# Late weight blocks by a list of products, and the loads of k, v and q one by one, in a fused attention and MLP kernel

## The chip, the cores and the metric

The kernel runs on one core of a Trainium2 chip. The metric is the device time of one execution in microseconds (us). Times of a kernel are medians of several runs; a profiled execution gives the trace.

## What is computed

The reference is linear attention with a normalisation, then two MLPs one behind the other, all in fp32 (cut to the lines that matter):

```python
kv  = einsum('bhsd,bhse->bhde', k, v)             # B=8, H=8, S=576, D=64
out = einsum('bhsd,bhde->bhse', q, kv)
att = out / sqrt(mean(out*out, -1) + 1e-6) * g_norm
x   = att as (4608, 512)
x   = (((x @ w1) * (x @ w2)) @ w3) @ w_out        # 512 -> 1024 -> 1024 -> 512
out = silu(x @ w_in) @ w_out2                     # 512 -> 2048 -> 512
```

## The kernel before

**Precision.** A matrix product runs as three passes of TensorE over operands split in a high and a low part: ScalarE makes the high part with a copy, VectorE the low part with a subtraction. The weights come from memory as packed words; two ScalarE operations and one VectorE operation unpack 128x512 of them.

**Two stages.** The first stage (trace, 73 to 469 us) works on token chunks `c` of 512. For the five chunks in `PLAIN` it runs the first MLP directly: 40 steps, each of two groups of 12 matmuls (`pa`, `pb`) and a third group for the second product (`x2ps`). Between the groups stand slots, six to a step, at which other work is begun (`event`, `att_step`, lines 669 to 700): the attention of the next chunks, that is `kv_load` and `q_load` (DMAs issued on SyncE), `kv_mm`, `att_a` and so on. The table `at_` (line 672) says how far behind the start of a chunk each part stands, in halves of which one is a slot; a chunk starts 27 slots after the last. Also in between, `pace` calls `advance` (line 299), one move of a pipeline that loads packed weights, splits them, forms sums of blocks and writes them to DRAM (`wbd`); its writes stand on SyncE's queue with a buffer of two tiles for each kind of sum.

The second stage (469 us to the end) runs the seven `UNITS`: units 0 and 1 (kind A) are the first MLP for the chunks that are left, units 2 to 6 (kind B) are the second MLP. Each matrix product is done by a seven-product scheme (Strassen-like): 52 blocks, seven products each, 12 matmuls in a product. In the text b2n3 is product 3 of block 2. The order of blocks is fixed by lines 710 to 715: unit 0's a0, b0, a1, b1, out0 are blocks 0 to 4, then unit 1's a0 (5), unit 0's out1 (6), unit 1's b0, a1, b1, out0 (7 to 10), unit 2's in0 (11), and so on.

**What a product waits for.** The results of a product land in PSUM; eight tiles go round, six to a block, two of them (one for each half `d`) for each of three banks. Products 0, 2, 4 and 6 use bank 0, product 1 bank 1, products 3 and 5 bank 2 (`RUNS`). Behind each product `post.after` has ScalarE copy a result out (products 0, 2, 3; in blocks of kind `a` also 6) or VectorE add it up. So ScalarE's copy of product 0 must be done before product 2 starts, that of 2 before 4, that of 3 before 5, and that of product 6 before product 1 of the next block, whose tiles are the same two. Every product also has a `w_load` behind it: SyncE waits until the product is done and refills its weight buffer, six products ahead of use.

**The late blocks.** Of the 16 blocks of the second MLP's weights, twelve are split in the first stage (`EARLY`) and four, 12 to 15, in the second stage, by the generator `late` (line 1009). It has eleven parts: (1) load the first half; (2) unpack it on ScalarE, two operations; (3) load the second half, finish the first on VectorE; (4) nothing; (5) unpack the second half on ScalarE; (6) finish it and form a sum on VectorE; (7) three more sums, one copy on ScalarE; (8) a copy and two low parts; (9) write four tiles, one copy and one low part; (10) another copy and low part, two writes; (11) the last two writes. The raw tile has one buffer (`LRAW`), the unpacked tiles `t0` and `t1` one each. `late_all` (line 1079) begins a block each seven parts (`LEVERY`), so that two blocks overlap in four parts; one part of each live block is issued ahead of each product in blocks whose name stands in `LATES`, that is blocks 0, 2, 4, 5 and the first products of 8.

The queues of the engines run in order: an instruction that waits holds up everything behind it on its engine.

Of the kernel before, what the change touches and what calls it, by code (L numbers as in the profile page):

```python
# [8 lines left out]
F32R = mybir.dt.float32r  # L9
U32 = mybir.dt.uint32  # L10
# [5 lines left out]
P = 128  # L16
B, H, S, D = 8, 8, 576, 64
# [5 lines left out]
N = 512  # L23
# [3 lines left out]
K2 = F2 // P  # L27
# [3 lines left out]
LATER = tuple(c for c in range(NCH) if c not in PLAIN)  # L31
UNITS = (("A", 512), ("A", 512), ("B", 512), ("B", 512), ("B", 512), ("B", 384), ("B", 384))
HMAX = max(w for _, w in UNITS)
HOP = 512
LRAW, LWH, LEVERY = 1, 3, 7
LATES = (("a", 0), ("a", 1), ("out", 0))
FIRST, PERIOD = 10, 13.5
EARLY = 12

NDB = {"A": K1 // 4, "B": K2 // 4}  # L40
WBD = {"in": 0, ("B", "out"): 4, "a": 8, "b": 10, ("A", "out"): 12}
# [38 lines left out]
def fused(ctx, tc, q, k, v, g, w1, w2, w3t, wo1, wb, out):  # L80
# [59 lines left out]
    for p in range(KD):  # L140
        r = 32 * p
# [455 lines left out]
    for x in ORDER.split():  # L597
        f = x.rstrip("0123456789")
# [26 lines left out]
        return [[(wch[4 * r + 2 * i + t][:, s], wcl[4 * r + 2 * i + t][:, s]) for r in range(2) for t in range(2)]  # L625
                for s in cols], wbd[WBD["A", "out"] + i][:, :, d]

    for n in range(K2):
        if n < EARLY:
            for role in range(3):  # L630
                pieces.append((wb[2 * n + role] if role < 2 else None, "block", role, wbd[n // 2][:, :, n % 2]))
        if n < 3 * K1 // 2:
            src, dst = resident(n)
            for role in range(3):
                pieces.append((src[role] if role < 2 else None, "sum", role, dst))
# [33 lines left out]
    def event(gap, f, *args):  # L669
        events.setdefault(int(2 * gap), []).append(lambda: f(*args))  # L670

    at_ = dict(k=4, q=7, a=4.5, a2=2.5, c=8, d=8.5, e=9.5, r=10.5)
    for c in range(1, NCH):
        gap = FIRST + PERIOD * (c - 2) - 4 * (c == B) if c > 1 else 1 - at_["a"]
        if 1 < c < B:
            event(gap, kv_mm, c, [0, 1, 2])
            event(gap, kv_load, c, [3, 4])
            event(gap + at_["k"], kv_mm, c, [3, 4])
            event(gap + at_["k"], kv_out, c)
        if c + 1 < B:  # L680
            event(max(gap + at_["k"], 2), kv_load, c + 1, [0, 1, 2])
        if c + 1 < NCH:
            for p in range(KD):
                event(gap + at_["q"], q_load, c + 1, p)
        for i in range(2):
            event(gap + at_["a"] + at_["a2"] * i, att_a, c, i)
            event(gap + at_["a"] + at_["a2"] * i, att_b, c, i)
        event(gap + at_["c"], att_c, c)
        event(gap + at_["d"], att_d, c)
        for f in (att_e, att_h, att_l):  # L690
            event(gap + at_["e"], f, c)
        for i in range(2):
            event(gap + at_["r"] + 2.5 * i, att_r, c, i)
            event(gap + at_["r"] + 2.5 * i, att_x, c, i)
            event(gap + at_["r"] + 2.5 + 2.5 * i + 0 * (c in LATER), att_f, c, i)

    def att_step(step, part):
        for n in range(6 * step + part - (part == 0), 6 * step + part + 1):
# [4 lines left out]
    def b_pool(name, **more):  # L703
        return ctx.enter_context(tc.tile_pool(name=name, **{**dict(bufs=1, reuse_waits="tile"), **more}))
# [10 lines left out]
    blocks.append((len(UNITS) - 1, "out", NDB[UNITS[-1][0]] - 1))  # L715
    stream = [(b, n) for b in range(len(blocks)) for n in range(7)]
    wt = {}

    def w_load(at):
        if at >= len(stream):  # L720
            return
        b, n = stream[at]
        u, which, i = blocks[b]
        from_ = w_rest if at % WBUFS else w_first
        t = from_.tile([P, 2, 2, 2 * P], F32, tag="w", name=f"w{b}_{n}")
        nc.sync.dma_start(out=t, in_=wbd[i + WBD[(UNITS[u][0], which) if which == "out" else which]][:, RUNS[n][1]])
        wt[b, n] = t
# [279 lines left out]
    lc = b_pool("lc")  # L1007

    def late(n):

        dst = wbd[n // 2][:, :, n % 2]

        def load(role):
            t = lc.tile([P, 2 * N], U32, tag="raw", bufs=LRAW, name=f"lraw{n}_{role}")
            nc.sync.dma_start(out=t, in_=wb[2 * n + role])
            return t.rearrange("p (n two) -> p n two", two=2)

        def scale(role, x):
            t = lc.tile([P, N], F32, tag=f"t{role}", name=f"lt{n}_{role}")
            z = lc.tile([P, N], U32, tag="wh", bufs=LWH, name=f"lz{n}_{role}")  # L1020
            nc.scalar.activation(out=t, in_=x[:, :, 1].bitcast(F32), func=AF.Prelu, scale=2.0 ** -112, alpha=-2.0 ** 32)
            nc.scalar.activation(out=z, in_=x[:, :, 0], func=AF.Copy, scale=0.93 * 2.0 ** -29)
            return t, z

        def bits(t, z):
            nc.vector.scalar_tensor_tensor(out=t.bitcast(U32), in0=t.bitcast(U32), scalar=3, in1=z,
                                           op0=ALU.logical_shift_left, op1=ALU.bitwise_or)

        def high(x):
            h = lc.tile([P, N], F32R, tag="wh", bufs=LWH, name=f"lh{n}")[:, :x.shape[-1]]  # L1030
            nc.scalar.copy(out=h, in_=x)
            return x, h

        def low(x, h):
            nc.vector.tensor_sub(out=x.bitcast(F32R), in0=x, in1=h.bitcast(F32))

        def write(op, x, h):
            o = x.shape[-1] // (2 * P)
            for i, y in ((0, h.bitcast(F32)), (1, x)):
                nc.sync.dma_start(out=dst[:, op:op + o, i, :], in_=y.rearrange("p (o c) -> p o c", c=2 * P))  # L1040

        raw = load(0)
        yield
        t0, z = scale(0, raw)
        yield
        raw = load(1)
        bits(t0, z)
        yield
        yield
        t1, z = scale(1, raw)  # L1050
        yield
        bits(t1, z)
        s12 = lc.tile([P, N], F32, tag="s12", name=f"ls12_{n}")
        s34 = lc.tile([P, N], F32, tag="s34", name=f"ls34_{n}")
# [12 lines left out]
        yield  # L1067
        write(A22, *x22)
        write(A11, *x1)
        x12 = high(s12)  # L1070
        low(*x12)
        yield
        x34 = high(s34)
        low(*x34)
        write(S1, *x12)
        yield
        write(S3, *x34)

    def late_all():
        todo = [late(n) for n in range(EARLY, K2)]  # L1080
        live = []
        at0 = 0
        while todo or live:
            if todo and at0 % LEVERY == 0:
                live.append(todo.pop(0))
            at0 += 1
            for x in list(live):
                if next(x, 0) == 0:
                    live.remove(x)
            yield  # L1090

    lates, LATE = late_all(), None
    gops = {}
    for b, (u, which, i) in enumerate(blocks):
        nxt = blocks[b + 1] if b + 1 < len(blocks) else None
        kind, w = UNITS[u]
        assert kind == "A" or (which, i) in (("in", 0), ("in", 1)) or LATE is not None
        post = {"in": Silu, "a": First, "b": Second, "out": Out}[which](b, u, i)
        ops = gops[u, i] if which == "out" else xops[u]
        more = u + 1 < len(UNITS)  # L1100
# [10 lines left out]
        if to_g:  # L1111
            gops[nxt[0], nxt[2]] = g_ops(nxt[0], nxt[2])
        for n in range(7):
            if (which, i) in LATES and next(lates, 0) == 0 and LATE is None:
                LATE = b
            if first and n < 3:
                ops.step(n + 4)
            if which == "out" and n + 3 < 7:
                ops.step(n + 3)
                if n + 3 == 6:  # L1120
                    held.append(ops.made[6])
            if steps and n >= 3:
                xops[u + 1].step(n - 3)
            if to_g:
                if n == (2 if first else 1):
                    for x in held:
                        nc.gpsimd.tensor_copy(out=gate, in_=x[:, 1, 0, :1].bitcast(F32))
                    held.clear()
                    gops[nxt[0], nxt[2]].sums()
                if n >= 4:  # L1130
                    gops[nxt[0], nxt[2]].step(n - 4)
            if n == sums_at:
                xops[u + 1].sums()
            if load:
# [57 lines left out]
```

## Time and profile before

| what | us |
|---|---|
| median of 3 runs (lowest to highest) | 1409.79 (1409.26 to 1409.94) |
| the profiled execution | 1409.83 |
| its span in the trace | 1408.0 |
| TensorE matmuls busy | 1378.2 |
| VectorE busy | 883.3 |
| ScalarE busy | 659.7 |
| GpSimd busy | 329.1 |

A busy share of an engine is a mean over both stages. Matmuls are pipelined, so that a busy TensorE is not one at its peak: the start-to-start time of its matmuls tells more. An engine's idle time ahead of an instruction is put down to what released it last.

### The profile page before, as it was taken

To read this page: it belongs to the slowest core of one execution; us is meant where nothing else is said; L and a number is where in the kernel's file an instruction comes from. 1 tells how busy PE (TensorE), PEld (TensorE's weight loads), DVE (VectorE), ACT (ScalarE), POOL (GpSimd) and SP (SyncE) were. 2 spreads that over 40 slices of the span, in tenths; PEclk is the share of its full clock that TensorE was granted. 3 is DMA by queue.
4 is the path that set the end of the run, shared out by engine and by line. 5 is a ranking of instruction groups with operands and counts; after the bars stand their busy time and mean duration, and the time that the engine had idled before them with its cause. 6 is when DMAs were issued, how large, how long until landed. Compare 5 with 4: busy or idle time off the path is not lost.

```text
span 1408.0 us, 19221 instructions
## 1 busy us (share of the span) xinstructions
PE 1378.2 (98%) x7012; PEld 1141.2 (81%) x7012; DVE 883.3 (63%) x1227; ACT 659.7 (47%) x1032; POOL 329.1 (23%) x206
## 2 busy tenths in 40 slices
PE   7999999999999999799999999999999999999998
PEld 4777777776778887688888888888888889999998
DVE  5854566567682476865774667545854576567458
ACT  5776445454552424522535354443535354544543
POOL 1000000000002040404532335124522442235222
PEclk9999999999999999999999999999999999999999
DMA  9755688988867497687677666866686668888886
GB/s 364 281 177 172 201 274 291 347 278 288 273 220 258 162 315 254 232 283 265 194 240 265 194 195 211 297 193 193 193 297 192 193 206 288 290 253 268 282 256 200
DMA packets 158157, 346.26 MB, mean 246 GB/s; under 512 B 15088, under 2 KB 73456, under 8 KB 158064
## 3 DMA queue, kind: packets, MB, share of 16 engines
q1 hardware_dynamic: 157488, 343.99, 74.1%
q8 instruction: 56, 0.92, 0.3%
q10 hardware_dynamic: 576, 1.05, 0.2%
q14 instruction: 37, 0.30, 0.1%
HBM read 270.53 MB, written 74.45 MB: 245 GB/s over the span
## 4 chain that ended last, share of the span: by engine, by line
PE 89%; DMA 5%; DVE 3%; ACT 2%; issue 1%; SPq 1%; DVEq 0%; ACTq 0%
PE ps L888 62%; PE wps L562 3%; PE pb L118 3%; PE x2ps L118 2%; PE pa L118 2%; PE pb L120 2%; PE pb L119 2%; PE x2ps L120 2%; PE x2ps L119 2%; PE pa L120 2%; PE pa L119 2%; PE kvps L342 1%; PE o L374 1%; DMA wbd<-w12l 1%; DMA v<-v_l 1%
## 5 line engine op out<-in xcount | busy, mean ns | idle before, releaser
L888 PE MATMUL ps<-xo,w 128*128 128x512 f32 (+1 forms) x2352 | 504.9, 375 | 8.9 <-ACT u L943 6.2
L888 PEld LDWEIGHTS ps<-xo,w 128*128 128x128 f32 x2352 | 433.8, 189 | 76.6 <-ACT u L943 7.0
L888 PE MATMUL ps<-go,w 128*128 128x512 f32 (+1 forms) x2016 | 426.2, 371 | 2.3 <-ACT c L991 1.3
L888 PEld LDWEIGHTS ps<-go,w 128*128 128x128 f32 x2016 | 368.4, 188 | 56.4 <-issue 2.0
L781 DVE TENSOR_TENSOR go<-g,go 128x1024 fp32r<-128x1024 f32 (+1 forms) x120 | 136.8, 1143 | 123.4 <-ACT go L780 122.1
L898 DVE TENSOR_TENSOR c<-ps,c 128x512 f32<-128x512 f32 (+1 forms) x280 | 170.8, 638 | 58.3 <-PE ps L888 56.1
L780 ACT CAST go<-g 128x1024 fp32r<-128x1024 f32 (+1 forms) x120 | 115.0, 978 | 50.6 <-PE ps L888 50.6
L768 POOL TENSOR_TENSOR x_t<-x2r 128x1024 f32<-128x1024 f32 (+1 forms) x14 | 32.6, 2329 | 436.1 <-DMA w<-wbd 435.6
L768 POOL TENSOR_TENSOR g_t<-g 128x1024 f32<-128x1024 f32 (+1 forms) x48 | 111.5, 2322 | 74.2 <-DVE g L970 69.3
L768 POOL TENSOR_TENSOR g<-g,g_t 128x1024 f32<-128x1024 f32 (+1 forms) x24 | 53.2, 2215 | 298.2 <-DVE go L781 298.2
L781 DVE TENSOR_TENSOR go<-g_t,go 128x1024 fp32r<-128x1024 f32 (+1 forms) x48 | 80.2, 1670 | 23.0 <-ACT go L780 23.0
L920 ACT COPY s<-ps 128x512 f32<-128x512 f32 (+1 forms) x40 | 21.7, 544 | 145.0 <-PE ps L888 145.0
L823 DVE TENSOR_TENSOR asb<-pb,asb 128x512 f32<-128x512 f32 x40 | 27.6, 690 | 84.0 <-PE pb L120 66.7
L898 DVE TENSOR_TENSOR g<-ps,s 128x512 f32<-128x512 f32 (+1 forms) x48 | 30.1, 642 | 68.0 <-PE ps L888 62.0
L113 ACT CAST ch<-asb 128x512 fp32r<-128x512 f32 x40 | 24.9, 624 | 92.6 <-DVE asb L823 92.6
L118 PE MATMUL x2ps<-ch,wch 128*128 128x512 f32 x160 | 65.0, 406 | 0.9 <-DVE x2o L655 0.9
L118 PE MATMUL pb<-xh,w12h 128*128 128x512 f32 x160 | 65.0, 406 | 0.0
L118 PE MATMUL pa<-xh,w12h 128*128 128x512 f32 x160 | 63.7, 398 | 0.0
L120 PE MATMUL x2ps<-ch,wcl 128*128 128x512 f32 x160 | 63.2, 395 | 0.0
L119 PE MATMUL x2ps<-cl,wch 128*128 128x512 f32 x160 | 63.0, 394 | 0.0
L120 PE MATMUL pb<-xh,w12l 128*128 128x512 f32 x160 | 62.5, 391 | 0.0
L119 PE MATMUL pb<-xl,w12h 128*128 128x512 f32 x160 | 62.4, 390 | 0.0
(139 smaller groups left out, 1760.4 us busy)
## 6 DMA issues: line engine op xcount, KB each, us to landing
w<-wbd SPq DMA_DIRECT2D x364, 512.0 KB, 4.4
wbd<-bh SPq DMA_DIRECT2D x60, 256.0 KB, 3.5
raw<-wb_l SPq DMA_DIRECT2D x24, 512.0 KB, 5.2
wbd<-s SPq DMA_DIRECT2D x48, 256.0 KB, 3.5
q<-q_l SPq DMA_DIRECT2D x36, 256.0 KB, 5.0
k<-k_l SPq DMA_DIRECT2D x32, 256.0 KB, 5.5
v<-v_l SPq DMA_DIRECT2D x32, 256.0 KB, 5.5
raw<-w_l SPq DMA_DIRECT2D x14, 512.0 KB, 4.5
```

The source lines that it names most:

```text
L113: nc.scalar.copy(out=h, in_=x)
L118: nc.tensor.matmul(out=ps_out, lhsT=ah, rhs=bh, start=first, stop=False)
L119: nc.tensor.matmul(out=ps_out, lhsT=ah, rhs=bl, start=False, stop=False)
L120: nc.tensor.matmul(out=ps_out, lhsT=al, rhs=bh, start=False, stop=last)
L562: nc.tensor.matmul(out=wps[m], lhsT=(l if which == "lh" else h)[:, x:x + P], rhs=rhs, start=left[m] == all_of, stop=left[m] == 1)
L768: nc.gpsimd.tensor_tensor(out=x, in0=x if a == place else self.src[a], in1=x if b == place else self.src[b], op=ALU.subtract)
L780: nc.scalar.copy(out=t[:, 0, :, :self.w], in_=x)
L781: self.cuts[n].tensor_tensor(out=t[:, 1, :, :self.w], in0=x, in1=t[:, 0, :, :self.w].bitcast(F32), op=ALU.subtract)
L823: nc.vector.tensor_mul(out=asb, in0=pb, in1=asb)
L888: mm = lambda a, bb, start, stop: nc.tensor.matmul(out=o, lhsT=a, rhs=bb, start=start, stop=stop, skip_group_check=True)
L898: eng.tensor_tensor(out=out_, in0=a, in1=b, op=ALU.add)
L920: nc.scalar.copy(out=t[nm, d], in_=o)
```

## The change

It has four parts. First, `LATES` becomes a list with a number for every product of the first blocks: so many parts of the late work are issued ahead of this product. Counted out, with the parts numbered on through each late block (part 11 of a block and part 1 of the next go together), the list gives:

| late block | part: product |
|---|---|
| 12 | 1: b0n0, 2: b0n2, 3: b0n3, 4 and 5: b0n4, 6: b1n0, 7: b1n1, 8: b1n2, 9: b1n6, 10: b2n1 |
| 13 | 1: b2n3, 2: b2n4, 3 and 4: b2n5, 5: b2n6, 6: b3n0, 7 and 8: b3n1, 9: b3n2, 10: b3n3 |
| 14 | 1: b4n4, 2: b6n2, 3 and 4: b6n6, 5: b7n3, 6: b8n0, 7: b8n1, 8: b8n5, 9: b8n6, 10: b9n0 |
| 15 | 1: b9n0, 2: b9n1, 3: b9n2, 4: b9n3, 5: b9n6, 6: b12n0, 7: b12n1, 8: b12n3, 9: b12n6, 10: b14n0, 11: b14n2 |

Second, `late_all` takes one late block at a time. Third, the order in which the first stage splits its twelve blocks becomes `NEED`; it is the same set of twelve, and the sums of resident tiles between them keep their places. Fourth, the loads of the attention move: in each chunk k and v of block 3 come 2 slots and those of block 4 come 4 slots after `kv_mm` of blocks 0 to 2 (both stood right behind it); blocks 0, 1 and 2 of the next chunk come 8, 10 and 12 slots after it (all stood at 8); q of pairs 0 and 1 comes at 17 slots and of pairs 2 and 3 at 22 (all stood at 14); the last part of the attention, `att_f`, comes one slot later. An assertion in `w_load` takes the place of the one in the block loop, and three named constants are written out as numbers.

```diff
-LRAW, LWH, LEVERY = 1, 3, 7
-LATES = (("a", 0), ("a", 1), ("out", 0))
+AT = dict(a=4.5, a2=2.5, k=4, l0=0, l1=1.0, l3=1, q=4.0, q1=0, c=8, d=8.5, e=9.5, r=10.5, r2=2.5, f=3.0)
+LATES = tuple(int(x) for x in """
+1011200 1110001 0101121 1211000 0000100 0000000
+0010002 0001000 1100011 2111001 0000000 0000000
+1101001 0000000 1010000 0011001 0100000 0100000
+0000000 0100000 0000000   
+""" if x.isdigit())
 EARLY = 12
+NEED = (0, 1, 2, 3, 8, 9, 4, 5, 10, 11, 6, 7, 12, 13, 14, 15)
...
-    for n in range(K2):
-        if n < EARLY:
+    for at_n, n in enumerate(NEED):
+        if at_n < EARLY:
...
+        n = at_n
...
-    at_ = dict(k=4, q=7, a=4.5, a2=2.5, c=8, d=8.5, e=9.5, r=10.5)
+    def place(c):
+        return FIRST + PERIOD * (c - 2) - 4 * (c == B)
...
             event(gap, kv_mm, c, [0, 1, 2])
-            event(gap, kv_load, c, [3, 4])
-            event(gap + at_["k"], kv_mm, c, [3, 4])
+            for i in range(2):
+                event(gap + AT["l3"] * (i + 1), kv_load, c, [3 + i])
+            event(gap + AT["k"], kv_mm, c, [3, 4])
...
-            event(max(gap + at_["k"], 2), kv_load, c + 1, [0, 1, 2])
+            for i in range(3):
+                event(max(gap + AT["k"] + AT["l0"] + AT["l1"] * i, 2), kv_load, c + 1, [i])
...
-                event(gap + at_["q"], q_load, c + 1, p)
+                event(gap + AT["a"] + AT["a2"] * (p // 2) + AT["q"] + AT["q1"] * (p % 2), q_load, c + 1, p)
...
-            event(gap + at_["r"] + 2.5 + 2.5 * i + 0 * (c in LATER), att_f, c, i)
+            event(gap + AT["r"] + AT["f"] + AT["r2"] * i, att_f, c, i)
...
     def late_all():
-        todo = [late(n) for n in range(EARLY, K2)]
-        live = []
-        at0 = 0
-        while todo or live:
-            if todo and at0 % LEVERY == 0:
-                live.append(todo.pop(0))
-            at0 += 1
-            for x in list(live):
-                if next(x, 0) == 0:
-                    live.remove(x)
-            yield
+        for n in NEED[EARLY:]:
+            yield from late(n)
+            undone.remove(n // 2)
...
         for n in range(7):
-            if (which, i) in LATES and next(lates, 0) == 0 and LATE is None:
-                LATE = b
+            for _ in range(LATES[7 * b + n] if 7 * b + n < len(LATES) else 0):
+                next(lates, None)
```

## Rows read from the trace of the kernel before

**Rows 1.** the page's busy time of TensorE over the span (part 1)

```profile
PE 1378.2 (98%) x7012; PEld 1141.2 (81%) x7012; DVE 883.3 (63%) x1227; ACT 659.7 (47%) x1032; POOL 329.1 (23%) x206
```

**Rows 2.** waits of TensorE by line: us in total, times, longest us

```profile
PE ps L888 <- ACT u L943: 6.2, 2, 5.6
...
PE rb L431 <- DVE rhl L421: 4.0, 3, 2.3
...
PE ps L888 <- DVE g L898: 2.7, 1, 2.7
...
PE kvps L342 <- DVE ob L438: 1.8, 2, 1.4
...
PE ps L888 <- ACT c L991: 1.3, 1, 1.3
...
PE x2ps L118 <- DVE x2o L655: 0.9, 1, 0.9
```

**Rows 3.** chain of work that ended last: start us, us, what

```profile
469.73 40.84 PE ps L888 x180
...
604.60 778.30 PE ps L888 x3720
...
1383.15 2.32 PE ps L888 x12
...
1385.67 18.98 PE ps L888 x108
```

**Rows 4.** windows: stretch, its us, busy us by engine, clock, DMA, GB/s

```profile
180.00:200.00 20.00, 17.72 (x70) 13.56 (x70) 15.66 (x28) 10.30 (x18) 0.00 (x0) 0.91 0.82 266
...
580.00:600.00 20.00, 13.12 (x44) 10.18 (x45) 15.91 (x18) 11.92 (x18) 4.85 (x3) 0.83 0.74 234
...
700.00:800.00 100.00, 100.00 (x443) 82.81 (x442) 59.99 (x67) 47.54 (x64) 27.52 (x13) 1.00 0.72 234
```

**Rows 5.** ScalarE timeline: start us, us, instruction [idle before <-releaser]

```profile
517.06 0.66 ACT L1021 ACTIVATE lt<-lraw 128x512 f32<-128x512 f32 x1 [5.36 <-DMA wbd<-lt]
...
523.23 0.68 ACT L1021 ACTIVATE lt<-lraw 128x512 f32<-128x512 f32 x1 [2.51 <-DMA lraw<-wb_l]
...
580.01 0.67 ACT L1021 ACTIVATE lt<-lraw 128x512 f32<-128x512 f32 x1 [6.50 <-DMA wbd<-lt]
...
583.54 1.06 ACT L943 COPY u<-ps 128x512 f32<-128x512 f32 x2
...
591.45 0.66 ACT L1021 ACTIVATE lt<-lraw 128x512 f32<-128x512 f32 x1 [5.87 <-DMA lraw<-wb_l]
```

**Rows 6.** the raw tile of the late blocks: its loads to landing

```profile
DMA to landing us min/median/max: 3.4/5.3/8.4
```

**Rows 7.** SyncE timeline, 170 to 176 us: start us, us, DMA issued

```profile
169.88 0.46 SPq L327 DMA_DIRECT2D k<-k_l  x1
...
174.03 0.33 SPq L327 DMA_DIRECT2D v<-v_l  x1
...
175.38 0.38 SPq L297 DMA_DIRECT2D wbd<-s  x1
```

**Rows 8.** VectorE timeline, 487 to 581: a quiet step, then steps beside GpSimd

```profile
487.05 0.42 DVE L1060 TENSOR_TENSOR ls<-lt,lt 128x256 f32<-128x256 f32 x1
...
572.73 2.62 DVE L1060 TENSOR_TENSOR ls<-lt,lt 128x256 f32<-128x256 f32 x1
...
575.60 5.38 DVE L1035 TENSOR_TENSOR lt<-lt,lh 128x256 fp32r<-128x256 f32 x2
```

**Rows 9.** costliest groups on the page: busy us, mean ns | idle before

```profile
L768 POOL TENSOR_TENSOR g_t<-g 128x1024 f32<-128x1024 f32 (+1 forms) x48 | 111.5, 2322 | 74.2 <-DVE g L970 69.3
```

**Rows 10.** VectorE timeline, 172 to 181 us

```profile
172.45 0.68 DVE L286 TENSOR_TENSOR s<-s,bh 128x512 fp32r<-128x512 f32 x1
...
180.90 0.42 DVE L253 TENSOR_TENSOR s<-t,t 128x256 f32<-128x256 f32 x1 [4.13 <-DMA wbd<-s]
```

**Rows 11.** DMA issues: count, KB each, median us to landing

```profile
k<-k_l SPq DMA_DIRECT2D x8, 128.0 KB, 3.7
```

More of the change, by code (lines that the diff above doesn't have):

```diff
@@ L670, in event @@
         events.setdefault(int(2 * gap), []).append(lambda: f(*args))
-    at_ = dict(k=4, q=7, a=4.5, a2=2.5, c=8, d=8.5, e=9.5, r=10.5)
+    def place(c):
+        return FIRST + PERIOD * (c - 2) - 4 * (c == B)
     for c in range(1, NCH):
-        gap = FIRST + PERIOD * (c - 2) - 4 * (c == B) if c > 1 else 1 - at_["a"]
+        gap = place(c) if c > 1 else 1 - AT["a"]
         if 1 < c < B:
             event(gap, kv_mm, c, [0, 1, 2])
-            event(gap, kv_load, c, [3, 4])
-            event(gap + at_["k"], kv_mm, c, [3, 4])
-            event(gap + at_["k"], kv_out, c)
+            for i in range(2):
+                event(gap + AT["l3"] * (i + 1), kv_load, c, [3 + i])
+            event(gap + AT["k"], kv_mm, c, [3, 4])
+            event(gap + AT["k"], kv_out, c)
         if c + 1 < B:
-            event(max(gap + at_["k"], 2), kv_load, c + 1, [0, 1, 2])
+            for i in range(3):
+                event(max(gap + AT["k"] + AT["l0"] + AT["l1"] * i, 2), kv_load, c + 1, [i])
         if c + 1 < NCH:
             for p in range(KD):
-                event(gap + at_["q"], q_load, c + 1, p)
+                event(gap + AT["a"] + AT["a2"] * (p // 2) + AT["q"] + AT["q1"] * (p % 2), q_load, c + 1, p)
         for i in range(2):
[L686 to L689, printed above, removed]
+            event(gap + AT["a"] + AT["a2"] * i, att_a, c, i)
+            event(gap + AT["a"] + AT["a2"] * i, att_b, c, i)
+        event(gap + AT["c"], att_c, c)
+        event(gap + AT["d"], att_d, c)
         for f in (att_e, att_h, att_l):
-            event(gap + at_["e"], f, c)
+            event(gap + AT["e"], f, c)
         for i in range(2):
-            event(gap + at_["r"] + 2.5 * i, att_r, c, i)
-            event(gap + at_["r"] + 2.5 * i, att_x, c, i)
-            event(gap + at_["r"] + 2.5 + 2.5 * i + 0 * (c in LATER), att_f, c, i)
+            event(gap + AT["r"] + AT["r2"] * i, att_r, c, i)
+            event(gap + AT["r"] + AT["r2"] * i, att_x, c, i)
+            event(gap + AT["r"] + AT["f"] + AT["r2"] * i, att_f, c, i)
     def att_step(step, part):
@@ L717, in fused @@
     wt = {}
+    undone = [n // 2 for n in NEED[EARLY:]]
     def w_load(at):
@@ L723, in w_load @@
         u, which, i = blocks[b]
+        assert UNITS[u][0] == "A" or i + (4 if which == "out" else 0) not in undone
         from_ = w_rest if at % WBUFS else w_first
@@ L1013, in load @@
         def load(role):
-            t = lc.tile([P, 2 * N], U32, tag="raw", bufs=LRAW, name=f"lraw{n}_{role}")
+            t = lc.tile([P, 2 * N], U32, tag="raw", bufs=1, name=f"lraw{n}_{role}")
             nc.sync.dma_start(out=t, in_=wb[2 * n + role])
@@ L1019, in scale @@
             t = lc.tile([P, N], F32, tag=f"t{role}", name=f"lt{n}_{role}")
-            z = lc.tile([P, N], U32, tag="wh", bufs=LWH, name=f"lz{n}_{role}")
+            z = lc.tile([P, N], U32, tag="wh", bufs=3, name=f"lz{n}_{role}")
             nc.scalar.activation(out=t, in_=x[:, :, 1].bitcast(F32), func=AF.Prelu, scale=2.0 ** -112, alpha=-2.0 ** 32)
@@ L1029, in high @@
         def high(x):
-            h = lc.tile([P, N], F32R, tag="wh", bufs=LWH, name=f"lh{n}")[:, :x.shape[-1]]
+            h = lc.tile([P, N], F32R, tag="wh", bufs=3, name=f"lh{n}")[:, :x.shape[-1]]
             nc.scalar.copy(out=h, in_=x)
@@ L1079, in late_all @@
     def late_all():
-        todo = [late(n) for n in range(EARLY, K2)]
-        live = []
-        at0 = 0
-        while todo or live:
-            if todo and at0 % LEVERY == 0:
-                live.append(todo.pop(0))
-            at0 += 1
-            for x in list(live):
-                if next(x, 0) == 0:
-                    live.remove(x)
-            yield
-    lates, LATE = late_all(), None
+        for n in NEED[EARLY:]:
+            yield from late(n)
+            undone.remove(n // 2)
+    lates = late_all()
     gops = {}
@@ L1096, in fused @@
         kind, w = UNITS[u]
-        assert kind == "A" or (which, i) in (("in", 0), ("in", 1)) or LATE is not None
         post = {"in": Silu, "a": First, "b": Second, "out": Out}[which](b, u, i)
```

## The prediction

> **What bounds the kernel now.** I read the page's busy times first. TensorE is busy for 1378.2 of 1408.0 us [rows 1], so the end moves only by what TensorE stands still for, or does at half clock. No transfer or other engine is the bound by its sum.
>
> Next come TensorE's waits by line [rows 2]. In the second stage (line 888) the waits are 6.2, 2.7 and 1.3 us, for ScalarE's copy `u`, VectorE's sum `g` and ScalarE's copy `c`. In the first stage, behind its prologue, they are 4.0 us (`rb`, for the last step of the normalisation), 1.8 (`kvps`, for a PSUM bank that VectorE frees) and 0.9 (`x2ps`): 6.7 us.
>
> Then I place them, by the chain of waits [rows 3]. The second stage has 52 x 7 x 12 = 4368 matmuls. Those from 604.60 on are 3720 + 12 + 108 = 3840, so 528 lie between 469.73 and 604.60. An undisturbed one takes 40.84 / 180 = 0.227 us, a product of 12 then 2.72. So 528 need 119.8 us and take 134.9: **15.1 us are lost in the first 44 products**, which are those among which the late parts stand. Behind them nothing is lost: a window from 700 to 800 has 100.00 us of TensorE at full clock [rows 4]. Blocks of the same kinds run there without late parts, so the other work of a block fits under its matmuls.
>
> The 15.1 contain a clock loss. From 580 to 600 the granted clock is 0.83, from 180 to 200 it is 0.91, after waits there [rows 4]: it fell from 2.4 to 1.2 GHz for part of each window. That costs 0.17 x 20 = 3.4 us in the second stage and 0.09 x 20 = 1.8 us in the first. The first stage's loss is thus 6.7 + 1.8 = **8.5 us**. More than 15.1 + 8.5 = 23.6 us is not to be had; the prologue (to 73 us) is hardly touched.
>
> **Where the 15.1 us come from.** ScalarE's queue is in order. Its first unpacking step for a late block stood idle before 517.06 and 580.01, for 5.36 and 6.50 us, until a write of `lt` had landed; the steps at 523.23 and 591.45 stood 2.51 and 5.87 us for the raw load [rows 5]. At 583.54, right behind, stand the copies `u` that TensorE wants. So two causes hold ScalarE: the next late block wants `t0` while the last one's is still being written (two blocks overlap, one buffer), and a raw load is unpacked one or two products after it is issued.
>
> **The list and one block at a time.** Nothing is added or left out: the same four blocks, the same instructions. What goes is the overlap. The write of `t0` is in part 9, the next unpacking in part 2 of the next block: in the list b1n6 to b2n4, b3n2 to b6n2, b8n6 to b9n1. The shortest has two products, 5.4 us, between them and the load in between besides, so the waits for writes should go. Blocks 4 and 5, where most of the loss is, keep a single load.
>
> What stays is the second cause, where load and unpacking stand close: b0n3 to b0n4, b2n3 to b2n4, b2n5 to b2n6, b9n0 to b9n1. A raw load takes 3.4 to 8.4 us to land, median 5.3 [rows 6]. Each place in turn:
> - b0n4: only products 5 and 6 follow, with ScalarE wanted at the end of 6; 5.3 us are over by then. Nothing.
> - b2n3 on: call its start T. SyncE first issues a weight load and two writes, each near 0.45 us [rows 7], so the raw load goes at T+1.3 and lands at T+6.6. Two unpackings of 0.66 each [rows 5] end at T+7.9. The one raw buffer is free then: the next load goes at T+8.0, lands at T+13.3, is unpacked at T+14.6. Behind it on ScalarE is the copy of product 6 (0.53 each half [rows 5]), done at T+15.2. Product 1 of block 3 wants that bank at T + 5 x 2.72 = T+13.6. So TensorE waits 1.6 us. With both landings at 4.4 us it is nothing; with both at 6.5 it is 4.0; with 8.4 twice it is 7.8.
> - b9n0: writes and the last low part come first, so that the load goes some 4 to 5 us into product 0, lands near 9.8, is unpacked at 11.1, and the copy of product 2 ends at 11.7 us after the start of block 9. Product 4 wants it at 10.9: 0.8 us, with bounds 0 and 4.
>
> On VectorE the parts that fall beside GpSimd's sums cost more: the same subtraction took 0.42 us at 487.05 and 2.62 at 572.73, and two low parts 5.38 [rows 8]; one GpSimd sum takes 2.3 us [rows 9]. In the list five such steps (parts 6 and 7 of block 14) stand in b8n0 and b8n1, where GpSimd runs. At some 2 us each, from these rows, VectorE is 10 us late, and has caught up when product 6 wants product 4's sum. I take nothing, with an upper end of 2 us.
>
> The Trainium skill's page "SBUF — State Buffer" (the section on which accesses contend) says that a VectorE operation with two SBUF inputs and a GpSimd operation that reads SBUF exclude each other for a whole instruction. That agrees with 2.62 against 0.42 [rows 8]. By it all five steps would wait one GpSimd sum each, some 14 us in all, and product 6 would be 0.7 us late: 1393.9 in place of the 1393.2 below.
>
> In blocks 6, 12 and 14, which had no late part, the pieces are one or two steps of 0.4 to 0.7 us to a product of 2.72. VectorE is nearly full in 6 and 12 but each sum has a product's length of grace; nothing, with an upper end of 1 us. What is left in the second stage: 1.6 + 0.8 = 2.4 us of 15.1. **Gain 12.7**, bounds 15.1 and 6.
>
> **The loads of k, v and q.** No DMA is added. What moves is where SyncE stands. At 169.88 to 174.03 it issues six loads for the next chunk in a row, four of them waiting for TensorE's `kv_mm`; behind them stands the write of a sum at 175.38 [rows 7]. Its data was ready at 172.45 + 0.68. VectorE stands 4.13 us before 180.90 for this very write, since the next sum wants the buffer [rows 10], and then the normalisation is late: `rb` waits 2.3 us [rows 2] and the clock falls for 1.8. With only one pair of loads ahead of it the write goes some 2.3 us earlier, at 173.1. VectorE's wait is cut by that, `rb`'s with it to about nothing, and the clock stays: gain 2.3 + 1.8 = 4.1, less 0.2 for what is left, **3.9**; bounds 0 (the queue is as long at that point) and 4.1.
>
> The other waits I leave: `rb`'s remaining 1.7 us follow from a chain of steps on VectorE and ScalarE that the change does not touch; `kvps` and `x2ps` wait for VectorE behind the write of `x2o`, whose place is the same. Upper end: their 2.7 us go too.
>
> The price is cover. k and v of block 4 now have 4 slots to their matmuls, two groups of 12, 5.4 us; they had 8 slots. They are half size, 3.7 us to land [rows 11], and are two issues on SyncE, 0.9 [rows 7]. 4.6 < 5.4: nothing, as long as SyncE is not over 0.8 us late. SyncE is late less often if it no longer stands waiting for TensorE. The other moved loads keep over 15 slots (k, v) or 11 (q, last chunk): hidden. `NEED` changes addresses; the first stage's steps are alike. `att_f` a slot later still stands two groups, 5.4 us, ahead of its use. Nothing for these.
>
> **The sum.** 1408.0 - 12.7 - 3.9 = 1391.4 of span. The profiled execution took 1409.83, 1.8 more than its span, and stands 0.04 over the median: **1393.2 us**.
>
> **Rivals.**
> - *All of it goes.* The landings are 4.4 us or less, and the bank and `x2o` waits go with the shorter queue. 23.6 less the 1.7 of `rb`: 21.9, so 1387.9. For: 3.4 is the fastest landing. Against: the median is 5.3.
> - *The close pairs still hold ScalarE.* Landings near 6.5 us: 4.0 at b3n1, 2.0 at b9n4, and one fall of the clock, 1.8: 7.8 in place of 2.4. Gain 11.2, so 1398.6. For: before 591.45 ScalarE did wait 5.87 us for such a load [rows 5]. The Trainium skill's page "DMA: Bandwidth & Descriptors" (rules for kernel authors) speaks for this rival: issue a DMA early and wait on it late. The list does the opposite at four places.
> - *Slower: the halved cover of k and v.* If SyncE comes to block 4's loads L late, each of six chunks has TensorE wait L - 0.8 us, and if that makes the clock fall, 1.8 more. It decides against the change from 6 x (L - 0.8 + 1.8) > 16.6, L over 1.8. With L = 3 it costs 24: 1417. Against: the queue is shorter than before.
> - *The list does not do what it is written for.* The waits in blocks 4 and 5 come from the blocks' own work, and stay: only the 3.9, so 1405.9. Against: the same kinds of blocks from 700 on lose nothing [rows 4].
>
> **How the numbers follow.** Forecast 0.48; all of it 0.22; close pairs 0.18; late k and v 0.06; the list does nothing 0.06. The forecast's own spread is 1390 to 1397. The range takes in the first two rivals and leaves out the last two (0.12) and the outer ends of the others (0.08): 1387 to 1401. About 0.2%, 2.8 us, is what can be told from no change. The last rival, at 3.9 us, lies near that bound: 0.03 of it counts as faster, 0.03 as the same. The slow rival gives 0.05 to slower and 0.01, a small L, to the same. Faster 0.48 + 0.22 + 0.18 + 0.03 = 0.91, same 0.04, slower 0.05.
>
> **What would show it.** In the trace of the changed kernel: no wait of ScalarE for a write of `lt`; TensorE without a gap in blocks 4 and 5; one gap near b3n1 for a ScalarE copy and a smaller one at b9n4, each behind an unpacking that waits for the raw load; no fall of the clock behind the prologue; `rb` waiting under 2 us in all; no wait of `kvps` for k or v behind the prologue. A wait of `kvps` for a DMA, or a new clock fall in blocks 2 to 9, would make it wrong.

## The result and the profile after

The changed kernel takes **1392.89 us**, the median of four runs (1391.14 to 1393.64), and the kernel before, in four runs on the same chip, 1409.87 (1409.26 to 1410.43). The ratio is 0.988, with a 95% interval of 0.986 to 0.990: 17.0 us, 1.2%. The profiled execution took 1392.65 us, with a span of 1390.8. The forecast was 1393.2, with a span of 1391.4.

In the page of the changed kernel the busy times of the other engines are those of before within 1%, but TensorE is busy 7.7 us less for the same 7012 matmuls [rows 1]. Some 5 us of that is the clock, by the shares of 0.83 and 0.91 that two windows of 20 us had before [rows 4] and that are 1.00 now.

```profile
PE 1370.5 (99%) x7012; PEld 1137.3 (82%) x7012; DVE 875.1 (63%) x1227; ACT 660.5 (47%) x1032; POOL 330.9 (24%) x206
```

The waits of TensorE behind the prologue are the second view (us in total, times, longest; the product line 888 is now 901, `rb` 431 is 437). The 6.2, 2.7 and 1.3 us of the second stage [rows 2] have shrunk to one wait of 0.7, and `rb` is down from 4.0 to 1.7. `kvps` waiting for VectorE, and `x2ps`, stand as they stood.

```profile
PE kvps L348 <- DVE ob L444: 1.8, 2, 1.4
PE rb L437 <- DVE rhl L427: 1.7, 2, 0.9
...
PE x2ps L124 <- DVE x2o L662: 1.0, 1, 1.0
PE ps L901 <- ACT u L976: 0.7, 1, 0.7
```

The windows that showed a clock loss before [rows 4] show none. The columns are busy time and count of TensorE's matmuls, of its weight loads, of VectorE, ScalarE and GpSimd, then the granted clock, the DMA share and GB/s:

```profile
180.00:200.00 20.00, 20.00 (x129) 15.60 (x128) 15.77 (x28) 11.72 (x21) 0.00 (x0) 1.00 0.95 325
...
580.00:600.00 20.00, 20.00 (x90) 16.57 (x89) 15.21 (x20) 5.95 (x8) 0.57 (x2) 1.00 0.75 235
```

Where the time went is read from the start times of single matmuls: the first of the first MLP ends the prologue, the first of line 888 or 901 ends the first stage, and products are counted off by twelves.

| stretch | before, us | after, us | gain | forecast |
|---|---|---|---|---|
| prologue | 73.0 | 72.8 | 0.2 | 0 |
| first stage | 396.5 | 393.1 | 3.4 | 3.9 |
| first 44 products of the second stage | 135.0 | 120.2 | 14.8 | 13.5 |
| from there to the end of block 14 | 166.0 | 166.9 | -0.9 | -0.8 |
| blocks 15 to 51 and the end | 637.4 | 637.8 | -0.4 | 0 |
| span | 1408.0 | 1390.8 | 17.2 | 16.6 |

### The profile page after: what moved, and what is told of

It reads as the page before. It is cut to its first block, busy times and chain, and to the rows that moved or that the text cites. A ratio compares the mean times of both kernels' runs of the same rounds, so it can differ in the third digit from the quotient of the medians.

```text
span 1390.8 us, 19194 instructions
## 1 busy us (share of the span) xinstructions
PE 1370.5 (99%) x7012; PEld 1137.3 (82%) x7012; DVE 875.1 (63%) x1227; ACT 660.5 (47%) x1032; POOL 330.9 (24%) x206
## 4 chain that ended last, share of the span: by engine, by line
PE 93%; DMA 4%; DVE 1%; ACT 1%; SPq 1%; issue 0%; DVEq 0%; ACTq 0%
PE ps L901 65%; PE pb L124 3%; PE wps L568 3%; PE x2ps L124 3%; PE pb L126 2%; PE pa L124 2%; PE pb L125 2%; PE x2ps L126 2%; PE x2ps L125 2%; PE pa L125 2%; PE pa L126 2%; PE kvps L348 1%; PE o L380 1%; DMA v<-v_l 1%; DMA x2d<-x2o 1%; PE s L399 1%
```

## Experiments

Every ratio is against runs of the kernel before on the same chip; over the chips that kernel's median lay between 1407.9 and 1409.9.

### The parts apart

**The list alone**, with a late block at a time, and the loads of k, v and q and `att_f` as before:

```diff
...
-            for i in range(2):
-                event(gap + AT["l3"] * (i + 1), kv_load, c, [3 + i])
+            event(gap, kv_load, c, [3, 4])
...
-            for i in range(3):
-                event(max(gap + AT["k"] + AT["l0"] + AT["l1"] * i, 2), kv_load, c + 1, [i])
+            event(max(gap + AT["k"], 2), kv_load, c + 1, [0, 1, 2])
...
-                event(gap + AT["a"] + AT["a2"] * (p // 2) + AT["q"] + AT["q1"] * (p % 2), q_load, c + 1, p)
+                event(gap + 7, q_load, c + 1, p)
```

> The list, one block at a time and NEED as in the change; the loads of k, v and q and att_f as in the kernel before. Theory: the second stage gives its 14 us back on its own, and the wait of rb behind a late write of sums stays. So about 1409.9 - 14 = 1396 us; in the trace no loss in blocks 4 and 5 of the second stage, and a rb wait of about 2.3 us near 187 us with a fall of the clock. Rival, that the two halves of the change need each other: over 1400, or under 1394 with the rb wait gone.

It took 1396.02 us against 1408.34, ratio 0.991 (0.990 to 0.993). In its trace the `rb` wait of before is back, and with it the fall of the clock. Its row in the waits of TensorE:

```profile
PE rb L437 <- DVE rhl L427: 3.9, 3, 2.2
```

and its window from 180 to 200, with the granted clock at 0.91:

```profile
180.00:200.00 20.00, 17.80 (x98) 13.52 (x98) 15.87 (x28) 10.33 (x19) 0.00 (x0) 0.91 0.77 248
```

Its second stage takes 289.6 us to the end of block 14, 2.5 more than that of the changed kernel, with the same list. The wait at block 9 is longer here, and the clock falls there too (0.91 from 640 to 660):

```profile
PE ps L899 <- ACT u L974: 1.8, 1, 1.8
```

**The loads alone** (and `NEED`), with the late blocks placed and overlapped as before:

```diff
...
     def late_all():
-        for n in NEED[EARLY:]:
-            yield from late(n)
-            undone.remove(n // 2)
+        todo = [late(n) for n in range(EARLY, K2)]
+        ...
+            if todo and at0 % LEVERY == 0:
+                live.append(todo.pop(0))
...
-            for _ in range(LATES[7 * b + n] if 7 * b + n < len(LATES) else 0):
-                next(lates, None)
+            if (which, i) in LATES and next(lates, 0) == 0 and LATE is None:
+                LATE = b
```

> The loads of k, v and q one by one and NEED as in the change; the late blocks overlapped and placed as in the kernel before. Theory: 3.9 us less than before, near 1406; VectorE's wait for the write of a sum near 178 us falls from 4.1 to about 1.2 us, rb's wait there goes, and the second stage still loses about 15 us. Rival, that the first stage's gain was chance: 1409 to 1411 with the rb wait still there.

It took 1405.29 us against 1408.34, ratio 0.998 (0.997 to 0.999). `rb` waits 1.7 us as in the changed kernel, and the second stage loses as before, most of it at one place, with the clock at 0.78 from 580 to 600. The row in its waits of TensorE:

```profile
PE ps L895 <- ACT u L950: 8.4, 1, 8.4
```

The two gains, 12.3 and 3.0 us, add up to 15.3, which agrees with the 17.0 of both within their intervals. `NEED` was not run by itself. In the first stage it gives nothing: with the old loads that stage takes 396.9 us with `NEED`, and 396.5 and 397.4 without it.

**Only the three loads of the next chunk one by one**, with everything else about k, v, q and `att_f` as before, beside the list:

```diff
-            for i in range(2):
-                event(gap + AT["l3"] * (i + 1), kv_load, c, [3 + i])
+            event(gap, kv_load, c, [3, 4])
             ...
             for i in range(3):
                 event(max(gap + AT["k"] + AT["l0"] + AT["l1"] * i, 2), kv_load, c + 1, [i])
```

> The changed kernel with the loads of k and v of blocks 3 and 4, of q and the place of att_f as before: of the first stage's edits only the spreading of the next chunk's blocks 0, 1 and 2 is left. Theory: this one edit lets the write of sums near 174 us out earlier, so rb's wait of 2.3 us near 186 us and the fall of the clock stay away, and the time is that of the changed kernel, 1392 to 1394 us. Rival, that the loads of blocks 3 and 4 or of q hold the queue: rb waits over 1.5 us there and the time is 1395 to 1397 us, that of the list alone.

1392.44 us against 1407.98, ratio 0.989 (0.986 to 0.991), `rb` at 1.7 us: the same as the whole change. So this one edit carries the first stage's gain (392.7 us in its trace, 393.1 in the changed kernel). Blocks 3 and 4, q and `att_f` add nothing that two runs can show.

### Which part of the list does it

**One late block at a time, nothing else**: the places stay those of the kernel before, and only the overlap of two late blocks goes.

```diff
     def late_all():
-        todo = [late(n) for n in range(EARLY, K2)]
-        live = []
-        at0 = 0
-        while todo or live:
-            ...
-            yield
+        for n in range(EARLY, K2):
+            yield from late(n)
```

> The kernel before with one edit: a late block begins when the last one has ended, still one part ahead of each product of blocks 0, 2, 4, 5, 8 and now 10. Theory: what holds ScalarE is mostly the write of the unpacked tile of the block before, so with the overlap gone the second stage loses 1 to 6 us of 15, for raw loads unpacked one product later: 1396 to 1401 us, and no wait of ScalarE for a write of lt. Rival, that the load pairs or the crowding of blocks 4 and 5 are the cause: 1404 us or more, with waits for lraw at the place of those for lt.

1405.56 us against 1408.34, ratio 0.998 (0.997 to 0.999). My theory, that the overlap with its waits for writes is the main cause, fell. ScalarE no longer waits for a write of `lt`, but TensorE still waits. ScalarE now stands for the raw loads, four times and 19.2 us in all, and TensorE for ScalarE. The two longest waits of TensorE, placed in its timeline and in ScalarE's (start, duration, engine, line, operation, and in brackets the idle time before it and what ended it):

```profile
569.56 0.66 ACT L1021 ACTIVATE lt<-lraw 128x512 f32<-128x512 f32 x1 [5.27 <-DMA lraw<-wb_l]
...
640.07 0.66 ACT L1021 ACTIVATE lt<-lraw 128x512 f32<-128x512 f32 x1 [5.84 <-DMA lraw<-wb_l]
...
572.24 14.25 PE L888 MATMUL ps<-xo,w 128*128 128x512 f32 x60 [3.13 <-ACT s L943]
...
641.81 26.41 PE L888 MATMUL ps<-xo,w 128*128 128x512 f32 x108 [2.75 <-ACT v L943]
```

At 569.56 ScalarE has stood 5.27 us for the raw load, and the copy of product 0 that TensorE wants for product 2 stands behind it. At 640.07 it is the copy of product 3. Up to the end of block 14 the second stage takes 296.3 us, 9.2 more than in the changed kernel. In this pair of traces taking the overlap away is thus worth 4.8 of the 14.0 us. But this execution was 1.9 us faster than the median of its ten: by the medians it is 2.8 us, with an interval of 0.8 to 3.9.

**The reverse: the list's places with the old overlap.**

```diff
     def late_all():
-        for n in NEED[EARLY:]:
-            yield from late(n)
-            undone.remove(n // 2)
+        todo = [late(n) for n in NEED[EARLY:]]
+        live = []
+        at0 = 0
+        while todo or live:
+            if todo and at0 % 7 == 0:
+                live.append(todo.pop(0))
+            ...
+            yield
```

> The changed kernel with the old overlap of the late blocks: each begins seven parts after the last, at the products of the list. ScalarE's waits for writes of lt are back, now at b1n6, b3n0 and b6n6. Theory: place decides; at b1n6 and b6n6 no copy of ScalarE is due for over 8 us and nothing is lost, at b3n0 the wait stands ahead of product 0's copies, which product 2 needs, and at b3n2 ahead of product 2's: 3 to 6 us in all, 1396 to 1399 us. Rival, that the overlap itself is the cost: all three waits reach TensorE, 10 us or more, over 1402 us.

1399.61 us against 1407.92, ratio 0.994 (0.992 to 0.995). Its ScalarE waits nearly twice as long for writes of `lt` as in the kernel before, and yet TensorE loses less. The row of the kernel before, then its own:

```profile
ACT lt L1021 <- DMA wbd<-lt: 16.0, 3, 6.5
...
ACT lt L1032 <- DMA wbd<-lt: 29.8, 3, 14.0
```

Its three waits, in the timelines of ScalarE and TensorE:

```profile
509.44 0.66 ACT L1032 ACTIVATE lt<-lraw 128x512 f32<-128x512 f32 x1 [10.55 <-DMA wbd<-lt]
...
511.17 19.33 PE L899 MATMUL ps<-xo,w 128*128 128x512 f32 x84 [0.18 <-ACT s L954]
...
531.46 0.66 ACT L1032 ACTIVATE lt<-lraw 128x512 f32<-128x512 f32 x1 [5.25 <-DMA wbd<-lt]
...
533.19 14.12 PE L899 MATMUL ps<-xo,w 128*128 128x512 f32 x60 [2.69 <-ACT s L974]
...
609.19 0.66 ACT L1032 ACTIVATE lt<-lraw 128x512 f32<-128x512 f32 x1 [13.99 <-DMA wbd<-lt]
...
611.45 38.74 PE L899 MATMUL ps<-xo,w 128*128 128x512 f32 x168 [1.57 <-ACT s L974]
```

10.55 us of ScalarE's waiting cost TensorE 0.18 us, and 13.99 cost 1.57, but 5.25 cost 2.69, at a place where the copy of product 0 was due. Thus ScalarE's waiting time is not the price of a late part. The price is by how much the wait outlasts the time until ScalarE's next copy is due.

To the end of block 14 this kernel takes 292.2 us, 5.1 more than the changed one. By the traces, then, the list's places alone bring 8.9 us of the second stage (301.1 to 292.2), one block at a time alone 4.8, and both 14.0. By the medians it is 5.3 (8.3 less the 3.0 of the loads), 2.8 and 12.3 (the list alone, which has both): neither part does it by itself.

**The same load and unpacking, two products earlier.** In block 2 the list's row is moved forward; the distance from the load to its unpacking stays one product:

```diff
-1011200 1110001 0101121 1211000 0000100 0000000
+1011200 1110001 0211200 1211000 0000100 0000000
```

> The changed kernel with the late parts of block 2 of the second stage two products earlier: load at b2n1, unpacking at b2n2, second load at b2n3, its unpacking at b2n4 (before: n3, n4, n5, n6). The lead from load to unpacking is the same one product. Theory: it counts where ScalarE waits, not how long; the wait now stands ahead of the copies of product 2, which product 4 needs, so TensorE waits 2 to 5 us there, perhaps with a fall of the clock: 1395 to 1400 us. Rival, that the lead decides: no more than 1 us over the changed kernel's 1393.

1398.51 us against 1407.98, ratio 0.993 (0.990 to 0.995), about 6 us over the changed kernel. The new row in its waits of TensorE:

```profile
PE ps L901 <- ACT u L956: 4.6, 1, 4.6
```

ScalarE's timeline at that place, and then the window around it, in which the clock falls:

```profile
515.98 0.66 ACT L1034 ACTIVATE lt<-lraw 128x512 f32<-128x512 f32 x1 [9.48 <-DMA lraw<-wb_l]
...
517.10 1.05 ACT L956 COPY u<-ps 128x512 f32<-128x512 f32 x2
```

```profile
500.00:520.00 20.00, 15.38 (x63) 12.33 (x62) 7.51 (x9) 4.93 (x9) 15.02 (x6) 0.90 0.88 283
```

Here the unpacking stands ahead of product 2's copy `u`, which product 4 needs. In the changed kernel it stands behind product 3's copy `v`, and no copy is due there until product 6 is done. ScalarE's timeline of the changed kernel:

```profile
515.12 0.59 ACT L956 COPY v<-ps 128x512 f32<-128x512 f32 x1 [0.77 <-PE ps L901]
520.54 0.67 ACT L1034 ACTIVATE lt<-lraw 128x512 f32<-128x512 f32 x1 [4.84 <-DMA lraw<-wb_l]
```

The place is not all that differs: ScalarE's wait is 9.48 us here and 4.84 there. The list puts one product between load and unpacking in both, but in time that is not the same. Here the load stands behind a write that SyncE issues late. It goes out 5.0 us into its product (which starts at 504.78), in the changed kernel 1.6 us into its product (which starts at 512.20). SyncE's rows, first of this kernel, then of the changed one:

```profile
509.35 0.36 SPq L1053 DMA_DIRECT2D wbd<-ls  x1
509.76 0.46 SPq L1028 DMA_DIRECT2D lraw<-wb_l  x1
...
513.76 0.54 SPq L1028 DMA_DIRECT2D lraw<-wb_l  x1
```

From the start of the load's product to the unpacking it takes 11.2 us here and 8.3 there. Without these 2.9 us about 1.7 of the 4.6 us would be left for the place, by my estimate from these rows.

The Trainium skill's page "DMA: Bandwidth & Descriptors" (rules for kernel authors) asks to issue a DMA early and to wait on it late. Here ScalarE begins to wait 3.3 us before the load goes out, in the changed kernel 1.9 us after it. So this run speaks for that rule and for the place alike, and does not part them. That the place decides is shown by the run with the old overlap.

### What was left, and the slower rival

**Block 9's unpacking two products later**, behind the copy `u`:

```diff
-0010002 0001000 1100011 2111001 0000000 0000000
+0010002 0001000 1100011 2001111 0000000 0000000
```

> The changed kernel with one edit: in block 9 the unpacking of late block 15 moves from product 1 to product 3, its second load and the empty part to products 4 and 5. Theory: ScalarE's wait of some 6 us for the raw load then stands behind the copies of product 2, and the last wait of TensorE in the second stage (0.8 to 1.3 us) goes: 1 us less than the changed kernel, perhaps too little to measure; in the trace no wait for ScalarE's u. Rival, that the wait only moves to the copies of product 3: no change.

1391.13 us (1390.85 to 1391.93) against 1407.92, ratio 0.988 (0.986 to 0.990). **The change once more**, beside it:

> The changed kernel once more, on the chip of the next two. About 1393 us.

1391.96 us (1391.15 to 1394.31), ratio 0.989 (0.987 to 0.990). The wait for `u` is there in the second (0.8 us) and gone in the first, where one of 0.3 us for `s` stands in block 3. The second stage to the end of block 14 takes 286.3 us in place of 287.1. The medians differ by 0.8 us, as they should, but their ranges overlap: by the times alone that isn't told apart. In the first the load also has two products more to land, so that the run does not part the place from the longer lead. Its median is the lowest of all that was run.

**That list, and the attention's part `e` half a unit (one slot) earlier**, to help `rb`:

```diff
-... c=8, d=8.5, e=9.5, r=10.5, r2=2.5, f=3.0)
+... c=8, d=8.5, e=9.0, r=10.5, r2=2.5, f=3.0)
```

> Meant to beat both: the changed kernel with the attention's step e (VectorE's two operations ahead of rb) one slot earlier, and in b9 the unpacking of late block 15 moved from product 1 to product 3, its second load to product 4. Theory: rb's two waits of 0.9 us go, since the steps run ahead of the split and the sums on VectorE, and ScalarE's wait at b9 stands where TensorE needs no copy (0.8 us): 2.5 us less than the changed kernel, near 1390.5. Rival, that VectorE's order only moves the wait (to x2ps or kvps): within 1 us of 1393.

1394.56 us against 1407.98, ratio 0.990 (0.987 to 0.992). All waits of `rb` are gone, and two others have taken their place. Its waits of TensorE:

```profile
PE x2ps L124 <- DVE x2o L662: 3.3, 1, 3.3
PE kvps L348 <- DVE ob L444: 2.5, 1, 2.5
```

The wait of `x2ps`, at 335, brings a fall of the clock that the changed kernel doesn't have, as the window shows:

```profile
320.00:340.00 20.00, 16.71 (x63) 12.24 (x62) 12.63 (x22) 8.56 (x17) 0.00 (x0) 0.85 0.83 269
```

So `rb`, `kvps` and `x2ps` compete for VectorE: with one earlier the others were late. The 4.5 us that remain of waits in the first stage are not to be had by moving one of them in this way.

**Less cover for k and v of blocks 3 and 4**, the slower rival driven on: block 4's loads stand two slots ahead of their matmuls in place of four.

```diff
-AT = dict(a=4.5, a2=2.5, k=4, l0=0, l1=1.0, l3=1, ...
+AT = dict(a=4.5, a2=2.5, k=4, l0=0, l1=1.0, l3=1.5, ...
```

> The changed kernel with k and v of blocks 3 and 4 another 1 and 2 slots later (3 and 6 after the first matmuls, used at 8). Block 4's loads then have one group of 12 (2.7 us) of cover in chunks 2, 4 and 6 and none in 3, 5 and 7, against 4.6 us to issue and land. Theory: kvps waits about 1.9 us three times and 4.6 us three times for v, 19 us, and the longer ones make the clock fall (up to 5 us): 1410 to 1418 us, slower than the kernel before. Rival, that the loads are hidden anyway, since SyncE runs ahead of TensorE: under 1397 us.

1426.29 us against 1407.98, ratio 1.013 (1.009 to 1.016), worse than I expected. The first stage takes 36 us more. Behind the prologue `kvps` waits five times for `v`, 26.6 us in all, and the clock falls at four of these waits. In the timeline of this kernel, three rows of SyncE and one of TensorE, it is seen why:

```profile
161.50 5.57 SPq L665 DMA_DIRECT2D x2d<-x2o  x4
...
168.13 0.47 SPq L333 DMA_DIRECT2D k<-k_l  x1
168.65 0.60 SPq L333 DMA_DIRECT2D v<-v_l  x1
...
172.15 1.12 PE L348 MATMUL kvps<-v,k 64*64 64x64 f32 x16 [9.38 <-DMA v<-v_l]
```

The window around it has the clock at 0.74:

```profile
160.00:180.00 20.00, 10.62 (x76) 7.88 (x75) 5.32 (x11) 2.79 (x7) 0.00 (x0) 0.74 0.94 306
```

In SyncE's timeline of the changed kernel the same two loads go out at 154.86 and 155.38, ahead of the writes of `x2o`:

```profile
154.86 0.47 SPq L333 DMA_DIRECT2D k<-k_l  x1
155.38 0.61 SPq L333 DMA_DIRECT2D v<-v_l  x1
...
161.63 5.64 SPq L665 DMA_DIRECT2D x2d<-x2o  x4
```

The four writes take SyncE 5.6 us, 3.7 of them standing ahead of the last one; ahead of an earlier write to `wbd` it stands 4.1 us. Moving the load by one group of matmuls, 2.7 us, puts it behind them, and it goes out 13 us later. The price is a jump and not a slope.

## Why the prediction held, step by step

The forecast was right in the sum and in its main mechanism: late parts hold up ScalarE and SyncE's row of loads holds up a write, and nearly all that TensorE lost by it goes. Step by step:

**The size of what can be had.** 528 undisturbed matmuls were to take 119.8 us; they take 120.2. Right.

**Where the 15.1 us come from.** I named two causes, the waits for writes and the close raw loads. Both are there. For the raw loads I asked place by place when ScalarE's next copy is due, and that was right; the waits for writes I took by their length. Length isn't what counts: in the changed kernel ScalarE still waits 16.5 us for raw loads, in four waits of up to 6.5, and in the kernel with the list and the old overlap 29.8 us for writes, for 5.1 us in the end (by the traces). What counts is what stands behind the wait: at block 2 the list puts it where no copy is due for three products. (At block 9 it doesn't, and that is the 0.7 us.)

A third cause I overlooked in the kernel before: VectorE beside GpSimd. The 6.50 us that ScalarE stood before 580.01 [rows 5] were for a write that SyncE issued only at 578.24, and that was 1.7 us in landing. Its data came late: VectorE's two low parts took 5.38 us from 575.60 on, beside GpSimd's sums [rows 8]; in block 8 of the changed kernel the same two take 1.01, when GpSimd is idle. Rows of SyncE and GpSimd before, and of VectorE after:

```profile
578.24 0.32 SPq L1040 DMA_DIRECT2D wbd<-lt  x1
...
575.34 2.59 POOL L768 TENSOR_TENSOR g_t<-g 128x1024 f32<-128x1024 f32 x1
...
633.23 1.01 DVE L1048 TENSOR_TENSOR lt<-lt,lh 128x256 fp32r<-128x256 f32 x2
```

In the kernel with the loads alone, too, 6.5 us of ScalarE's waiting ahead of TensorE's 8.4 are put down to VectorE. The list takes these steps out of block 5, where GpSimd forms sums. No run moves them by themselves, so how much of the 14.0 us is owed to that stays open.

**Block 3, product 1: this step failed.** I forecast 1.6 us for the two unpackings at b2n4 and b2n6. They came where I had them, but by luck. The first load went out 1.6 us into product 3 (which starts at 512.2), where I had 1.3, and its unpacking began 8.3 us into it, where I had 6.6; the second load went out at 9.6 (I had 8.0), and its unpacking began at 13.2 (I had 13.3). So the first took about 6.7 us to land and the second 3.5, where I had 5.3 for each. Both halves of product 6's copy were done at 15.3; my 15.2 was for the first. TensorE did not wait. In ScalarE's timeline below, the copies of product 6 start at 526.49; product 1 of block 3 starts at 525.8, in the middle of TensorE's row without a gap from 499.73 to 542.46.

```profile
525.37 0.66 ACT L1034 ACTIVATE lt<-lraw 128x512 f32<-128x512 f32 x1 [3.62 <-DMA lraw<-wb_l]
...
526.49 1.06 ACT L958 COPY g<-ps 128x512 f32<-128x512 f32 x2
...
499.73 42.73 PE L901 MATMUL ps<-xo,w 128*128 128x512 f32 x187
```

The wrong step is the sentence that product 1 wants that bank; it stands ahead of the prediction too, where product 1 of the next block is said to have the same two tiles as product 6. The PSUM tiles do not go round in a fixed turn: in the trace product 1 of blocks 1, 2 and 3 has a wait for its weights alone and none for ScalarE, and in block 3 it starts before the copy does. In what order the tiles are handed on is not shown. The wait that the close pair can cause is one product on, for the copy of product 0 behind that of product 6: it is 0.3 us in the kernel with block 9's unpacking moved, and nothing in the changed kernel.

**Block 9, product 4.** 0.8 us forecast, 0.7 measured, by the mechanism named: the raw load went out 3.7 us into the block (I had 4 to 5), ScalarE stood 6.46 us for it, and the copy `u` behind it came late. With the unpacking behind `u` the wait is gone. That it was 0.7 is in part luck: in other traces with this list at block 9 it is 0.8 (twice), 1.1, 1.2 and 1.8, the last with a fall of the clock for which I had set nothing here. The rows are ScalarE's and TensorE's of the changed kernel:

```profile
647.77 0.67 ACT L1034 ACTIVATE lt<-lraw 128x512 f32<-128x512 f32 x1 [6.46 <-DMA lraw<-wb_l]
...
648.88 1.06 ACT L976 COPY u<-ps 128x512 f32<-128x512 f32 x2
...
649.51 8.50 PE L901 MATMUL ps<-xo,w 128*128 128x512 f32 x36 [0.67 <-ACT u L976]
```

**VectorE beside GpSimd in block 8.** Nothing was forecast, and nothing came: four sums took 2.5 to 2.6 us each in place of 0.42 [rows 8], the step ahead of them 1.12, and TensorE's row runs on to 648.84. The four sums agree with the exclusion in the Trainium skill's page "SBUF — State Buffer" (section "Who interferes with whom"). By it I had worked out 0.7 us for product 6; that did not come. VectorE's rows of the changed kernel, one of the GpSimd sums beside them, and TensorE's row:

```profile
620.61 2.62 DVE L1070 TENSOR_TENSOR ls<-lt 128x256 f32<-128x256 f32 x1
623.26 2.50 DVE L1072 TENSOR_TENSOR ls<-ls,lt 128x256 f32<-128x256 f32 x1
625.68 2.62 DVE L1073 TENSOR_TENSOR ls<-lt,lt 128x256 f32<-128x256 f32 x1
628.23 2.62 DVE L1074 TENSOR_TENSOR ls<-lt,ls 128x256 f32<-128x256 f32 x1
...
620.22 2.73 POOL L781 TENSOR_TENSOR g<-g 128x1024 f32<-128x1024 f32 x1
...
599.72 49.12 PE L901 MATMUL ps<-xo,w 128*128 128x512 f32 x216
```

**The loads.** The write of the sum was to go at 173.1 and went at 173.57, before at 175.38 [rows 7]. VectorE's wait for it fell from 4.13 us [rows 10] to 1.23, and `rb` there waits no more. Row of SyncE, row of VectorE:

```profile
173.57 0.45 SPq L303 DMA_DIRECT2D wbd<-s  x1
...
178.27 0.43 DVE L259 TENSOR_TENSOR s<-t,t 128x256 f32<-128x256 f32 x1 [1.23 <-DMA wbd<-s]
```

The gain in this pair of traces is 3.4 us where I had 3.9. Over more traces the size is right: with the old loads the first stage took 396.5, 396.9 and 397.4 us, and in seven traces with the new loads of blocks 0 to 2 of the next chunk (without the two kernels that change other times of the attention) 392.7 to 393.1. The means differ by 4.0.

**The waits that I left**: `rb` 1.7, `kvps` 1.8 and `x2ps` 0.9 were to stay; they are 1.7, 1.8 and 1.0.

**The rivals.** That all of it goes did not come, since those 4.5 us stayed; of the second stage alone nearly all went. The close pair of block 2 held ScalarE but not TensorE, that of block 9 held both, for 0.7 us. The slower rival's mechanism is real, as the run with less cover shows, but the change has its loads ahead of the writes. My price for it, six times a lateness L, missed that L jumps when the load falls behind a write that waits.

That the sum came out to 0.3 us is luck, by small errors of both signs: 1.3 us too little for the second stage, 0.5 too much for the first in this pair of traces, and 0.4 us at the end that went the other way.

## What to carry to other kernels

Where an engine that runs in order must wait for something, ask which of its later results is due next and when: put the wait right behind the last one that is due soon, and its length costs nothing until the next. When an engine stands for a write, follow the write back to the engine that makes its data. On a DMA queue look at what stands in front, above all at writes and loads that wait for an engine: one issue more or less ahead of such a one moves a transfer by many microseconds, for better (the write of the sum, 1.8 us earlier) or worse (k and v, 13 us later). When a wait is removed by moving a step of an engine that others share, look whether it has come back under another name before you count it.

## What the runs showed of the hardware that I had not expected

The same 512 KB raw load, issued by the same queue, takes 3.5 to 7.5 us to land in the changed kernel. A wait of TensorE doesn't always cost clock: after 2.69 us at block 3 of the kernel with the list and the overlap the granted clock stayed 1.00 from 520 to 560; after 2.75 us at block 8 of the kernel with one late block at a time, and after 1.81 us at block 9 of the kernel with the list alone, it was 0.91 from 640 to 660. And the prologue of kernels that are alike there took 70.7 to 74.2 us in the traces, so that a difference of some 2 us between two single profiled executions is no evidence on a later stage; stage times are.
